# First MLP's weight halves kept in DRAM, and a float64 narrowing that takes its sign from a parametric ReLU

## The chip, the cores and the metric

The kernel runs on one core of one Trainium2 chip. A core has TensorE (PE, the matrix engine; PEld is its weight load), VectorE (DVE), ScalarE (ACT), GpSimd (POOL) and SyncE (SP), which issues all of this kernel's DMAs on one queue. Each engine works its instructions off in the order in which they were laid down, and semaphores tie the engines together. The metric is the time of one execution on the device in microseconds (us); the kernel before has a median of 1067.25 us over 3 runs (1065.96 to 1068.76).

## The reference, cut to what matters

```python
def _attn_ref(q_l, k_l, v_l, q_g, k_g, v_g):      # 4 batches, 8 heads, 512 local + 32 global tokens, head 64
    ...                                            # local window of 32 and global tokens, softmax
def _moe_ref(x, w_gate, w_val, w_out, rms_g):      # 2304 tokens, 512 wide, 1536 hidden
    rms = np.sqrt(np.mean(x * x, axis=-1, keepdims=True) + 1e-06)
    xn = x / rms * rms_g
    g = xn @ w_gate
    silu = g * (1.0 / (1.0 + np.exp(-g)))
    val = xn @ w_val
    return (silu * val @ w_out).astype(np.float32)
def _moe2_ref(x, w_in, w_out):                     # 512 wide, 2048 hidden
    h = x @ w_in
    g = np.maximum(0.01 * h, h)
    return (g @ w_out).astype(np.float32)
```

Attention, then a gated MLP, then a second MLP with a leaky ReLU. The weights of both MLPs come as float64 numbers; everything else is float32.

## The kernel before, in words

Each large matmul is done as three in the type float32r: every float32 operand is *split* into a high half (a rounding cast) and a low half (the operand minus the high half), and `mm3` (line 68) adds up high·high, low·high and high·low. `split` (line 85) makes a weight's high half on ACT (line 75) and its low half on POOL (line 83); the low halves of activations are made on DVE from the second block on, in the first block on POOL.

A float64 weight must first become a float32. `narrow` (line 93) gets the raw words of a 128x512 tile. ACT scales the upper word, read as a float32, by a power of two (line 104, tile `nc`, function Copy). DVE or POOL makes three low bits from the lower word (lines 109 and 106, tile `nr`). DVE shifts `nc` left by three and ORs the bits in (line 111), and a further DVE instruction ORs the sign bit in (line 112, tile `wf`, or `wfb` for the second MLP).

The first MLP takes the 2304 tokens in five blocks (512 and four times 416), and in each block 12 steps, one for each 128 hidden units. Step g uses three weights: k = 0 the gate (`pg` matmuls), k = 1 the value (`pv`), k = 2 the output (`yp` matmuls, which run in the next step). Beside blocks 0, 1 and 2 run the matmuls and softmax of the attention of batches 1, 2 and 3; block 3 has nothing beside it; block 4 has `ahead`: 12 weights of the second MLP are narrowed and split, and the first rows of the second MLP's input are read back and split.

In block 0 `convert` (line 495) narrows weight (g, k), starts the raw fetch of the next step into the one buffer `w64k` of that k, and stores the narrowed float32 tile `wf` to `w1_dram` (line 508). Blocks 1 to 4 fetch that tile (line 493, 256 KB) instead of narrowing again. In every block `prep` (line 510) then splits `wf` into the tiles `w0h`, `w0l` and so on, each with two buffers. `prep(g + 1, ...)` runs in step g, so a weight is split one step ahead and fetched two steps ahead.

The second MLP takes the tokens in five blocks with 16 steps each (`ph` matmuls, then `o`); between them ACT and DVE make `tl` and its halves `h2h` and `h2l`. All its 32 weights stay in the on-chip memory (SBUF). `weights2` (line 575) fetches, narrows and splits one: 12 in `ahead`, through three raw buffers, the other 20 in the second MLP's first block, through the two buffers of the tag `w64`.

The order on each engine is laid down by a scheduler that the program's order and its own estimate of time steer.

Of the kernel before, what the change touches and what calls it, by code (L numbers as in the profile page):

```python
# [8 lines left out]
F32 = mybir.dt.float32  # L9
F32R = mybir.dt.float32r  # L10
U32 = mybir.dt.uint32
AF = mybir.ActivationFunctionType
ALU = mybir.AluOpType
# [3 lines left out]
P = 128  # L17
# [6 lines left out]
def tile_window_global_attention_two_mlps(  # L24
# [10 lines left out]
    nc = tc.nc  # L35
    B, NP = kqv.shape[:2]
    _, _, KB, NT, _ = v_b.shape
# [6 lines left out]
    DM = NP * P  # L44
    KC = NP
    NF1 = w1.shape[0]
# [5 lines left out]
    scale = 1.0 / float(D) ** 0.5  # L52
# [4 lines left out]
    pools = [ph_ps.enter_context(tc.tile_pool(name="ps0", bufs=1, space=PSUM)), 8]  # L57
    dram = ctx.enter_context(tc.tile_pool(name="dram", bufs=1, space=bass.MemoryType.DRAM))
    y_dram = dram.tile([P, KC, NTOK], F32, name="y_dram")
    w1_dram = [[dram.tile([P, DM], F32, name=f"w1_dram{k}_{f}") for k in range(3)] for f in range(NF1)]  # L60
    ph1 = ctx.enter_context(ExitStack())
    mp = ph1.enter_context(tc.tile_pool(name="mp", bufs=1))
    ph_at = ExitStack()
# [9 lines left out]
    def high(eng, hi, src):  # L73
        if eng == "act":
            return nc.scalar.copy(hi, src)  # L75
        elif eng == "pool":
            nc.gpsimd.tensor_scalar(out=hi, in0=src, scalar1=1.0, scalar2=0.0, op0=ALU.mult, op1=ALU.add)
        else:
            nc.vector.tensor_copy(hi, src)
# [5 lines left out]
    def split(hi, lo, src, e_hi, e_lo):  # L85
        high(e_hi, hi, src)
        low(e_lo, lo, src, hi)
# [5 lines left out]
    def narrow(pool, dst, raw, name, e_r="dve"):  # L93

        c = pool.tile([P, DM], F32, tag="nar_c", bufs=2, name="nc_" + name)
        r = pool.tile([P, DM], U32, tag="nar_r", bufs=2, name="nr_" + name)
        cu = c.bitcast(U32)
        nc.scalar.activation(out=c, in_=raw[:, :, 1].bitcast(F32), func=AF.Copy, scale=2.0 ** -112)
        if e_r == "pool":
            nc.gpsimd.tensor_scalar(out=r, in0=raw[:, :, 0], scalar1=0.93 * 2.0 ** -29, scalar2=0.03,
                                    op0=ALU.mult, op1=ALU.add)
        else:
            nc.vector.tensor_scalar(out=r, in0=raw[:, :, 0], scalar1=2.0 ** -29, scalar2=7.0,  # L109
                                    op0=ALU.mult, op1=ALU.min)  # L110
        nc.vector.scalar_tensor_tensor(out=r, in0=cu, scalar=3, in1=r, op0=ALU.logical_shift_left, op1=ALU.bitwise_or)  # L111
        nc.vector.scalar_tensor_tensor(out=dst.bitcast(U32), in0=cu, scalar=0x80000000, in1=r,  # L112
                                       op0=ALU.bitwise_and, op1=ALU.bitwise_or)

    anchors = {}

# [360 lines left out]
    NI = len(BLOCKS1)  # L477
    wraw, wf, wsp = {}, {}, {}

    def step_of(g):  # L480
        return divmod(g, NF1)

    def fetch(g, k):

        i, f = step_of(g)
        if i >= NI:
            return
        if i == 0:
            wraw[g, k] = mp.tile([P, DM, 2], U32, tag=f"w64{k}", name=f"w64{k}_{f}")
            nc.sync.dma_start(out=wraw[g, k], in_=words(w1[f])[:, k])  # L490
        else:
            wf[g, k] = mp.tile([P, DM], F32, tag=f"wf{k}", bufs=2, name=f"wf{k}_{g}")
            nc.sync.dma_start(out=wf[g, k], in_=w1_dram[f][k])

    def convert(g, k):
        i, f = step_of(g)
        if i:
            return
        wf[g, k] = mp.tile([P, DM], F32, tag=f"wf{k}", bufs=2, name=f"wf{k}_{g}")
        with pinned({0: f"n{2 * NP - 1}", 1: "sqrt"}.get(f, "")):  # L500
            narrow(mp, wf[g, k], wraw[g, k], f"{k}_{f}", "pool" if k and f > 1 else "dve")
        if step_of(g + 1)[0] == 0:
            if g == 0:
                with tc.issue_after(loads[5, 1].ins):
                    fetch(g + 1, k)
            else:
                fetch(g + 1, k)
        nc.sync.dma_start(out=w1_dram[f][k], in_=wf[g, k])

    def prep(g, k):  # L510

        if step_of(g)[0] < NI:
            wsp[g, k] = [mp.tile([P, DM], F32R, tag=f"w{k}{y}", bufs=2, name=f"w{k}{y}_{g}") for y in "hl"]
            split(wsp[g, k][0], wsp[g, k][1], wf[g, k], "act", "pool")
        convert(g + 1, k)
        if step_of(g + 2)[0]:
            fetch(g + 2, k)

    cols = [sum(BLOCKS1[:i]) for i in range(NI)]
    yp = {}  # L520
# [75 lines left out]
    def mlp1(early):  # L596
# [8 lines left out]
        for g in range(NI * NF1):  # L605
            i, f = step_of(g)
# [4 lines left out]
            raw = g == 0  # L611
# [23 lines left out]
            for k in range(2):  # L635
                pp[k] = bank(f"p{'gv'[k]}_{g}")
                for c in range(KC):
                    mm3(pp[k][:, 0:n], [w[:, c * P:(c + 1) * P] for w in wsp[g, k]], [y[:, c, 0:n] for y in x],
                        c == 0, c == KC - 1)
                    if c == 1:  # L640
                        flush()
                        if k == 0:
                            prep(g, 2) if g else None
                        else:
                            prep(g + 1, 0)
                        between(2 * k)
                flush()
                if k == 0:
                    th = mp.tile([P, NX], F32, tag="th", bufs=2, name=f"th_{g}")
                    hs = [mp.tile([P, NX], F32R, tag=f"hs{y}", bufs=2, name=f"hs{y}_{g}") for y in "hl"]  # L650
                    t, hh, hl = (z[:, 0:n] for z in [th] + hs)
                    gate = pp[0][:, 0:n]
                    if raw:
                        gate = mp.tile([P, NX], F32, tag="gate", name="gate")[:, 0:n]
                        nc.vector.tensor_tensor(out=gate, in0=pp[0][:, 0:n], in1=norms[0][3]["rv"][:, 0:n], op=ALU.mult)
                    nc.scalar.activation(out=t, in_=gate, func=AF.Tanh, scale=0.5)  # L656
                    nc.vector.scalar_tensor_tensor(out=t, in0=t, scalar=1.0, in1=gate, op0=ALU.add, op1=ALU.mult)  # L657
                else:
                    nc.vector.scalar_tensor_tensor(out=t, in0=t, scalar=0.5, in1=pp[1][:, 0:n], op0=ALU.mult, op1=ALU.mult)
                    if raw:  # L660
                        nc.gpsimd.tensor_tensor(out=t, in0=t, in1=norms[0][3]["rv"][:, 0:n], op=ALU.mult)
                    high("act", hh, t)
                    later(lambda t=t, hh=hh, hl=hl: low("pool" if i < 1 else "dve", hl, t, hh))
                between(2 * k + 1)
            for m in range(2):
                if pend:
                    out_half(*pend, 2 * m)
                else:
                    flush()
                if m == 0:  # L670
                    prep(g + 1, 1)
                between(4 + m)
            pend = (g, [hh, hl])
        return pend
# [133 lines left out]
```

## Time and profile before

| | |
|---|---|
| median of 3 runs | 1067.25 us |
| the profiled execution | 1066.59 us |
| its span, first to last instruction | 1064.8 us |
| PE busy | 1002.9 us, 94% |
| DVE busy | 597.2 us, 56% |
| ACT busy | 481.4 us, 45% |
| POOL busy | 367.8 us, 35% |
| DMA moved | 116.33 MB, 109 GB/s over the span |
| granted PE clock, mean over the span | 0.977 of 2.4 GHz |

The profile shows one execution. For each engine it has the busy time, the time of each instruction, and for each idle time the instruction whose semaphore ended it ("hsl waits for hsh"). A line of a helper, such as 83, stands for many tiles, so a group is named by the tile it writes. Busy time of PE is that of matmuls which overlap: two that follow each other at 187 ns are shown with some 350 ns each, so PE's pace is read from counts in a stretch.

By the tiles, block 0 runs from about 57 to 219 us, blocks 1 to 3 to about 560 us, block 4 to 666 us, and the second MLP from there to the end.

### The profile page before, as it was taken

The numbers are of one execution on the slowest core, as the hardware profiler recorded it, in microseconds if no ns is written. First come the engines' busy times: TensorE is split into PE (matmuls) and PEld (weight loads), VectorE is DVE, ScalarE is ACT, GpSimd is POOL, SyncE is SP. The second block draws the span as 40 slices with busy tenths as digits, with TensorE's granted clock in tenths as the row PEclk, the third lists the DMA queues.
The fourth block names the chain that finished last, engine by engine and source line by source line (L and its number), as shares of the span: only waits on it lengthen the run. The fifth ranks groups of instructions, "written<-read, shape, count | busy, mean of one in ns | idle before, by whom it ended". The sixth has DMA issues, their size and how long they took to land.

```text
span 1064.8 us, 14868 instructions
## 1 busy us (share of the span) xinstructions
PE 1002.9 (94%) x5324; PEld 846.6 (80%) x5324; DVE 597.2 (56%) x1104; ACT 481.4 (45%) x1111; POOL 367.8 (35%) x283
## 2 busy tenths in 40 slices
PE   5968889999999999999997789988999999999998
PEld 4736667778888888899997689866888888888997
DVE  5899987366553866446349963599322232232232
ACT  4765556465554655455446543455222232232232
POOL 2468654543334443346557664244000000000000
PEclk8978999999999999999998999999999999999999
DMA  7556876633334442225345641453010010010000
GB/s 226 169 172 216 299 225 198 200 109 126 113 114 125 122 114 70 78 82 151 119 110 183 213 121 38 151 167 110 25 51 1 1 65 1 0 50 1 1 31 21
DMA packets 55452, 116.33 MB, mean 109 GB/s; under 512 B 8657, under 2 KB 11729, under 8 KB 55377
## 3 DMA queue, kind: packets, MB, share of 16 engines
q1 hardware_dynamic: 55376, 115.37, 34.6%
q8 instruction: 42, 0.69, 0.3%
q14 instruction: 34, 0.27, 0.1%
HBM read 97.00 MB, written 18.35 MB: 108 GB/s over the span
## 4 chain that ended last, share of the span: by engine, by line
PE 71%; DVE 7%; issue 4%; DMA 3%; ACT 1%; POOL 1%; DVEq 0%; SPq 0%; ACTq 0%
PE ph L71 15%; PE o L71 15%; PE yp L71 11%; PE pg L71 11%; PE pv L71 10%; PE po L257 2%; PE sc L213 2%; DMA w64b<-w 2%; PE pp L245 2%; DVE nr_b L109 1%; DVE wfb L112 1%; PE pz_g L320 1%; PE sa_g L279 1%; DVE nr_b L111 1%; DVE xl L83 1%
## 5 line engine op out<-in xcount | busy, mean ns | idle before, releaser
L733 DVE TENSOR_TENSOR tl<-ph,tl 128x512 f32<-128x512 f32 (+2 forms) x80 | 48.7, 609 | 153.8 <-ACT tl L732 153.5
L83 POOL TENSOR_TENSOR w0l<-wf,w0h 128x512 fp32r<-128x512 f32 x60 | 86.9, 1448 | 120.8 <-ACT w0h L75 116.8
L71 PE MATMUL ph<-ysph,w0l 128*128 128x512 f32 (+2 forms) x320 | 115.6, 361 | 0.0
L71 PE MATMUL ph<-yspl,w0h 128*128 128x512 f32 (+2 forms) x320 | 115.4, 360 | 0.0
L71 PE MATMUL ph<-ysph,w0h 128*128 128x512 f32 (+2 forms) x320 | 115.2, 360 | 0.0
L732 ACT ACTIVATE tl<-ph 128x512 f32<-128x512 f32 (+2 forms) x80 | 42.6, 533 | 160.1 <-PE ph L71 157.8
L83 POOL TENSOR_TENSOR w2l<-wf,w2h 128x512 fp32r<-128x512 f32 x60 | 88.2, 1470 | 70.7 <-ACT w2h L75 70.2
L71 PE MATMUL o<-w1h,h2l 128*128 128x512 f32 x272 | 107.6, 396 | 3.6 <-DVE h2l L83 3.5
L71 PE MATMUL o<-w1l,h2h 128*128 128x512 f32 x272 | 106.7, 392 | 0.0
L83 POOL TENSOR_TENSOR w1l<-wf,w1h 128x512 fp32r<-128x512 f32 x60 | 82.0, 1366 | 64.7 <-ACT w1h L75 58.6
L71 PE MATMUL pg<-xh,w0h 128*128 128x416 f32 (+1 forms) x236 | 90.2, 382 | 11.8 <-ACT w1h L75 7.2
L71 PE MATMUL yp<-hsh,w2h 128*128 128x416 f32 (+1 forms) x240 | 92.3, 389 | 4.8 <-ACT hsh L75 4.8
L71 PE MATMUL pg<-xh,w0l 128*128 128x416 f32 (+1 forms) x236 | 87.9, 372 | 2.3 <-POOL w0l L83 2.3
L71 PE MATMUL yp<-hsh,w2l 128*128 128x416 f32 (+1 forms) x240 | 89.5, 373 | 0.0
L71 PE MATMUL yp<-hsl,w2h 128*128 128x416 f32 (+1 forms) x240 | 81.7, 370 | 7.8 <-DVE hsl L83 7.8
L71 PE MATMUL o<-w1h,h2h 128*128 128x512 f32 x272 | 84.1, 398 | 5.0 <-ACT h2h L75 5.0
L71 PE MATMUL pg<-xl,w0h 128*128 128x416 f32 (+1 forms) x236 | 87.6, 371 | 0.3 <-DVE xl L83 0.2
L71 PE MATMUL pv<-xh,w1h 128*128 128x416 f32 (+1 forms) x236 | 86.5, 367 | 0.0
L71 PE MATMUL pv<-xl,w1h 128*128 128x416 f32 (+1 forms) x236 | 84.9, 360 | 0.0
L71 PE MATMUL pv<-xh,w1l 128*128 128x416 f32 (+1 forms) x236 | 84.5, 358 | 0.0
L83 DVE TENSOR_TENSOR h2l<-tl,h2h 128x512 fp32r<-128x512 f32 (+2 forms) x80 | 49.4, 618 | 50.0 <-ACT h2h L75 48.5
L657 DVE SCALAR_TENSOR_TENSOR th<-th,pg 128x416 f32<-128x416 f32 (+1 forms) x59 | 35.5, 601 | 73.1 <-ACT th L656 73.1
(149 smaller groups left out, 2219.3 us busy)
## 6 DMA issues: line engine op xcount, KB each, us to landing
wf<-w_dram SPq DMA_DIRECT2D x144, 256.0 KB, 2.7
w<-w SPq DMA_DIRECT2D x36, 512.0 KB, 4.6
w64b<-w SPq DMA_DIRECT2D x32, 512.0 KB, 4.3
kq<-kqv SPq DMA_DIRECT2D x32, 352.0 KB, 4.2
w_dram<-wf SPq DMA_DIRECT2D x36, 256.0 KB, 3.3
va<-kqv SPq DMA_DIRECT2D x16, 256.0 KB, 3.5
out<-ob SPq DMA_DIRECT2D x16, 256.0 KB, 2.1
y_dram<-ys SPq DMA_DIRECT2D x16, 208.0 KB, 2.5
```

The lines of the kernel that those rows point to most:

```text
L71: nc.tensor.matmul(dst, lhs[a], rhs[b], start=first and i == 0, stop=last and i == 2)
L83: e.tensor_tensor(out=lo, in0=src, in1=hi.bitcast(F32), op=ALU.subtract)
L109: nc.vector.tensor_scalar(out=r, in0=raw[:, :, 0], scalar1=2.0 ** -29, scalar2=7.0, op0=ALU.mult, op1=ALU.min)
L111: nc.vector.scalar_tensor_tensor(out=r, in0=cu, scalar=3, in1=r, op0=ALU.logical_shift_left, op1=ALU.bitwise_or)
L112: nc.vector.scalar_tensor_tensor(out=dst.bitcast(U32), in0=cu, scalar=0x80000000, in1=r, op0=ALU.bitwise_and, op1=ALU.bitwise_or)
L213: nc.tensor.matmul(sc[j][:, i * KW:(i + 1) * KW], kq[r, 2 * KW + i * P:2 * KW + (i + 1) * P], kq[r, i * KW:(i + 1) * KW], start=True, stop ...
L245: nc.tensor.transpose(pp[:, n * P:(n + 1) * P], s[:, c0:c0 + P], ident)
L257: nc.tensor.matmul(po[d, i * P:(i + 1) * P], v[0:rows, t, d], hold[j][0:rows, (n + i) * P:(n + i + 1) * P], start=n == 0, stop=n == 2)
L279: nc.tensor.matmul(sa[0:G2, 2 * h * P:2 * (h + 1) * P], q, k, start=True, stop=True)
L657: nc.vector.scalar_tensor_tensor(out=t, in0=t, scalar=1.0, in1=gate, op0=ALU.add, op1=ALU.mult)
L732: nc.scalar.activation(out=tl[:, 0:n], in_=pp[:, 0:n], func=AF.Copy, scale=0.01)
L733: nc.vector.tensor_tensor(out=tl[:, 0:n], in0=pp[:, 0:n], in1=tl[:, 0:n], op=ALU.max)
```

## The change

Three things. `narrow` loses the DVE instruction of line 112: ACT's function becomes a parametric ReLU with the slope −2^32 for negative inputs, so a negative number leaves it as a positive one with its exponent raised by 32, and the shift left by three moves that bit into the sign's place; line 111 then writes the result. In block 0 both halves of a weight lie in one tile of 128x2x512, and that tile (512 KB) is stored to DRAM, in `prep`, directly behind the split, no longer `wf` at the end of `convert`. In blocks 1 to 4 that tile is loaded ready (512 KB), at three places of step g for step g + 2, and nothing is split. The tile has three buffers for each k; the narrowed `wf` has one ring of five in place of two for each k.

```diff
-    w1_dram = [[dram.tile([P, DM], F32, name=f"w1_dram{k}_{f}") for k in range(3)] for f in range(NF1)]
+    w1_dram = [[dram.tile([P, 2, DM], F32, name=f"w1_dram{k}_{f}") for k in range(3)] for f in range(NF1)]
...
-        cu = c.bitcast(U32)
-        nc.scalar.activation(out=c, in_=raw[:, :, 1].bitcast(F32), func=AF.Copy, scale=2.0 ** -112)
+        nc.scalar.activation(out=c, in_=raw[:, :, 1].bitcast(F32), func=AF.Prelu, scale=2.0 ** -112,
+                             alpha=-2.0 ** 32)
...
-        nc.vector.scalar_tensor_tensor(out=r, in0=cu, scalar=3, in1=r, op0=ALU.logical_shift_left, op1=ALU.bitwise_or)
-        nc.vector.scalar_tensor_tensor(out=dst.bitcast(U32), in0=cu, scalar=0x80000000, in1=r,
-                                       op0=ALU.bitwise_and, op1=ALU.bitwise_or)
+        nc.vector.scalar_tensor_tensor(out=dst.bitcast(U32), in0=c.bitcast(U32), scalar=3, in1=r,
+                                       op0=ALU.logical_shift_left, op1=ALU.bitwise_or)
...
+    def weight_tile(g, k):
+
+        t = mp.tile([P, 2, DM], F32R, tag=f"w{k}", bufs=3, name=f"w{k}_{g}")
+        wsp[g, k] = [t[:, 0, :], t[:, 1, :]]
+        return t
+
     def fetch(g, k):
...
         else:
-            wf[g, k] = mp.tile([P, DM], F32, tag=f"wf{k}", bufs=2, name=f"wf{k}_{g}")
-            nc.sync.dma_start(out=wf[g, k], in_=w1_dram[f][k])
+            nc.sync.dma_start(out=weight_tile(g, k).bitcast(F32), in_=w1_dram[f][k])
+
+    def fetch_halves(g, k):
+        if step_of(g)[0]:
+            fetch(g, k)
 
     def convert(g, k):
         i, f = step_of(g)
         if i:
             return
-        wf[g, k] = mp.tile([P, DM], F32, tag=f"wf{k}", bufs=2, name=f"wf{k}_{g}")
+        wf[g, k] = mp.tile([P, DM], F32, tag="wf", bufs=5, name=f"wf{k}_{g}")
...
-        nc.sync.dma_start(out=w1_dram[f][k], in_=wf[g, k])
 
     def prep(g, k):
 
-        if step_of(g)[0] < NI:
-            wsp[g, k] = [mp.tile([P, DM], F32R, tag=f"w{k}{y}", bufs=2, name=f"w{k}{y}_{g}") for y in "hl"]
-            split(wsp[g, k][0], wsp[g, k][1], wf[g, k], "act", "pool")
-        convert(g + 1, k)
-        if step_of(g + 2)[0]:
-            fetch(g + 2, k)
+        i, f = step_of(g)
+        if i == 0:
+            t = weight_tile(g, k)
+            split(t[:, 0, :], t[:, 1, :], wf[g, k], "act", "pool")
+            nc.sync.dma_start(out=w1_dram[f][k], in_=t.bitcast(F32))
+            convert(g + 1, k)
...
                             prep(g + 1, 0)
+                        fetch_halves(g + 2, k)
                         between(2 * k)
...
                     prep(g + 1, 1)
+                else:
+                    fetch_halves(g + 2, 2)
                 between(4 + m)
```

## Rows read from the trace of the kernel before

**Rows 1.** The page: PE's busy us, share, instructions; then its tenths in 40 slices.

```profile
PE 1002.9 (94%) x5324; PEld 846.6 (80%) x5324; DVE 597.2 (56%) x1104; ACT 481.4 (45%) x1111; POOL 367.8 (35%) x283
...
PE   5968889999999999999997789988999999999998
```

**Rows 2.** Stretches: length, each engine's busy us (instructions), PE clock, DMA share, GB/s.

```profile
60.00:100.00 40.00, 29.57 (x125) 19.42 (x123) 39.74 (x65) 23.73 (x56) 28.09 (x20) 0.79 0.53 174
100.00:140.00 40.00, 36.70 (x195) 27.89 (x195) 39.22 (x70) 24.05 (x61) 28.58 (x19) 0.96 0.86 283
...
220.00:550.00 330.00, 329.57 (x1960) 292.45 (x1959) 186.60 (x402) 174.42 (x441) 144.21 (x108) 1.00 0.38 111
500.00:540.00 40.00, 40.00 (x214) 39.76 (x213) 14.79 (x19) 16.68 (x31) 23.55 (x19) 1.00 0.43 124
570.00:630.00 60.00, 42.71 (x200) 39.52 (x199) 52.92 (x56) 31.40 (x60) 45.15 (x32) 0.91 0.58 190
680.00:760.00 80.00, 71.45 (x292) 54.68 (x291) 64.44 (x85) 37.81 (x65) 30.60 (x20) 0.98 0.37 124
780.00:860.00 80.00, 80.00 (x347) 64.88 (x346) 20.80 (x32) 18.87 (x32) 0.00 (x0) 1.00 0.03 8
```

**Rows 3.** PE's waits, 550 to 760 us: us in total, times, longest.

```profile
PE yp L71 <- DVE hsl L83: 7.8, 5, 3.1
PE pg L71 <- ACT w1h L75: 7.2, 1, 7.2
```

**Rows 4.** Waits of the DMA queue (SP), the whole span.

```profile
SPq L493 <- POOL w0l L83: 121.1, 40, 8.4
...
SPq L578 <- DVE nr_b L109: 52.6, 23, 4.9
SPq L508 <- DVE wf L112: 43.5, 18, 6.9
```

**Rows 5.** Groups by shape: count, busy us, mean ns, idle before and its releasers.

```profile
L83 POOL TENSOR_TENSOR w0l<-wf,w0h 128x512 fp32r<-128x512 f32 x60 | 86.9, 1448 | 120.8 <-ACT w0h L75 116.8 <-DVE sq L433 3.2 <-POOL nr L106 0.6
...
L75 ACT CAST w0h<-wf 128x512 fp32r<-128x512 f32 x60 | 36.7, 611 | 0.0
...
L112 DVE SCALAR_TENSOR_TENSOR wf<-nc,nr 128x512 uint32<-128x512 uint32 x36 | 33.7, 950 | 6.8 <-POOL w2l L83 3.5 <-POOL w0l L83 2.9
...
L104 ACT ACTIVATE nc<-w 128x512 f32<-128x512 f32 x36 | 24.1, 672 | 28.4 <-issue 11.6 <-DVE wf L112 11.4 <-DMA w<-w 2.8
```

**Rows 6.** The tile hsl on DVE: ns min/median/max, first and last start.

```profile
L83 DVE TENSOR_TENSOR hsl<-th,hsh x48: 573/1274/1667, 237.9 to 665.6; 128x416 fp32r<-128x416 f32 x48
```

**Rows 7.** The page's DMA issues: count, size, median us from issue to landing.

```profile
w<-w SPq DMA_DIRECT2D x36, 512.0 KB, 4.6
w64b<-w SPq DMA_DIRECT2D x32, 512.0 KB, 4.3
```

**Rows 8.** DMA in 60 to 140 us: packets, the queue's share of 16 engines, issues.

```profile
DMA packets 6753, 18.28 MB, mean 229 GB/s; under 512 B 751, under 2 KB 751, under 8 KB 6746
...
q1 hardware_dynamic: 6746, 18.21, 69.3%
...
w_dram<-wf SPq DMA_DIRECT2D x20, 256.0 KB, 4.0
```

**Rows 9.** Groups of DVE in 570 to 630 us, columns as in rows 5.

```profile
L112 DVE SCALAR_TENSOR_TENSOR wfb<-nc_b,nr_b 128x512 uint32<-128x512 uint32 x10 | 13.2, 1315 | 2.4 <-POOL w0l L83 2.4
L109 DVE TENSOR_SCALAR nr_b<-w64b 128x512 uint32<-128x512 uint32 x8 | 11.4, 1421 | 0.0
```

**Rows 10.** DVE in order of time: start, us, instruction, idle before it.

```profile
680.53 0.43 DVE L109 TENSOR_SCALAR nr_b<-w64b 128x512 uint32<-128x512 uint32 x1 [3.97 <-DMA w64b<-w]
```

**Rows 11.** Groups of DVE in 680 to 742 us.

```profile
L112 DVE SCALAR_TENSOR_TENSOR wfb<-nc_b,nr_b 128x512 uint32<-128x512 uint32 x20 | 20.1, 1006 | 0.0
```

**Rows 12.** Groups of DVE in 60 to 140 us.

```profile
L112 DVE SCALAR_TENSOR_TENSOR wf<-nc,nr 128x512 uint32<-128x512 uint32 x21 | 19.7, 951 | 0.1
```

**Rows 13.** Groups by shape again: ACT's table loads ahead of Sqrt.

```profile
L461 ACT ACT_TABLE_LOAD x5 | 6.4, 1283 | 2.8 <-PE pm L458 2.7
```

## The prediction

> **What bounds the kernel now.** I read the page's busy shares first: TensorE (PE) is busy 94% of the span, so PE sets the time and only its idle time can be won. Its busy tenths fall below 9 in slices 1, 3 to 6, 22 to 24, 27 and 28 (and at the end) [rows 1]; those are the places to look at. The table of stretches gives the sizes [rows 2]. From 220 to 550 us (blocks 1 to 3 of the first MLP) PE idles 0.43 us of 330: nothing is to be had there. Three stretches fall short:
> - Block 0, where the first MLP's weights are narrowed beside attention: PE idles 10.4 us in 60 to 100 us and 3.3 us in 100 to 140, 13.7 together, while DVE is busy 79 of the 80 us.
> - Block 4, where the second MLP's first weights are narrowed: 570 to 630 us runs 200 matmuls. The undisturbed pace of the same shape is 214 in 40 us (500 to 540), 187 ns each, so the 200 are worth 37.4 us: 22.6 us are lost.
> - The second MLP's first block, with 20 more narrowings: 680 to 760 us runs 292 matmuls. The pace of 780 to 860 is 347 in 80 us, 231 ns each: 67.3 us of work, 12.7 us lost.
>
> Then what PE waits for between 550 and 760 us [rows 3]: the longest names are DVE's hsl and ACT's w1h. The first is DVE work served in its turn; the second is a split, fed by a fetch in the DMA queue, whose largest wait on POOL is 121.1 us for the low half w0l [rows 4]. So what stalls PE is two lists of work, DVE's and POOL's, that are served in order, and not the weights' bytes.
>
> **Part 1: a narrowing has one DVE instruction less (L112 goes), and ACT's Copy becomes Prelu.** Each of the first MLP's 36 takes 950 ns, 34 us of DVE together [rows 5]; the 32 of the second MLP are counted below by stretch. The trace has no Prelu. The nearest row is the Copy it replaces, 672 ns [rows 5]; the cast on the same 128x512 shape takes 611 [rows 5], so functions lie some 60 ns apart. I take no difference, with bounds of −60 and +60 ns: 2 us either way over 36, on an ACT that is busy 24 of 40 us [rows 2].
>
> **Part 2: blocks 1 to 4 load finished halves.** Removed: 48 × 3 = 144 splits. Of w0 the trace has 60 (12 of block 0, 48 later), 611 ns on ACT and 1448 ns on POOL [rows 5], and w1 and w2 have a group like it each: 88 us of ACT and 208 us of POOL go. In blocks 1 to 3 neither is on PE's path, so the gain there is 0. What the splits cost shows on DVE: hsl, with two operands in SBUF, takes 573 ns at least and 1274 in the median [rows 6], and DVE is busy only 14.8 of 40 us in block 3 [rows 2], so it isn't its own queue; I take it that a POOL split beside it holds it up, the other engine that reads the same memory then. PE covers that in block 3, not in block 4.
>
> Added: each load moves 512 KB, not 256: 144 × 262,144 B = 37.7 MB. Block 3 is the tightest: 3 × 524,288 B in a step of 36 matmuls × 187 ns = 6.73 us. In 500 to 540 us the DMA engines' share is 0.43 at 124 GB/s [rows 2], 288 GB/s when full, so a step's loads take 5.5 us of 6.73 and fit. With three buffers a load for step g+2 starts once step g−1 has released its tile: a lead of two steps, 13.5 us, against a landing of 4.6 us for 512 KB [rows 7]. Cost 0, covered by that lead; what it costs without is a rival below. The load waits for PE's reads now, no longer for POOL; in the SP queue behind it stand the stores of y and the raw loads, which have no reader in that step.
>
> **Part 3: block 0 stores the halves.** 36 stores grow by 262,144 B, 9.4 MB. They also move: from behind the next raw fetch to ahead of it, directly behind the split. SP then waits for POOL's low half, where it now waits for DVE's wf (43.5 us in 18 waits [rows 4]). Queued behind that wait are the raw fetch and the attention's loads. The raw fetch has to wait for the narrowing that reads its buffer, and on ACT that stands behind the same split, so I take 0 for the wait; the bytes are costed below.
>
> **The sum, stretch by stretch.**
> Block 4. DVE works 52.9 us in 570 to 630 [rows 2]. Ten of L112, at 1315 ns [rows 9], are 13.2 us of it. POOL runs 32 instructions there [rows 2]; about ten are splits of the second MLP (one for each of these narrowings) and stay, two thirds go. The 8 nr_b at 1421 ns [rows 9] took 430 ns undisturbed [rows 10], so 7.9 us of them is lengthening; two thirds, 5.3, go too. DVE falls to about 34 us, under the 37.4 us of matmuls, so PE becomes the bound. The turn in DVE's list still delays some steps: I leave 5.6 of 22.6. Gain 17, bounds 12 (L112 alone) and 22.6.
> The second MLP's first block. Twenty of L112 at 1006 ns [rows 11] leave DVE's 64.4 us [rows 2]. The next thing late is the ring of two w64 buffers: a landing of 4.3 us [rows 7] and a read of 0.7 (nc [rows 5]) make 5.0 us for two, 2.5 each, 50 us for 20 where 680 to 742 us are spent now. So DVE's 20 us can't all come back: 12 at most, and as DVE will wait for DMA with tl and h2l queued behind, I take 8. Bounds 4 and 12.7.
> [...]
> Block 0. 21 of L112 at 951 ns [rows 12], 20 us, leave a DVE that is full in 60 to 140 us: DVE alone would allow all 13.7 us. DMA moved 18.28 MB there at a share of 69.3% [rows 8], 330 GB/s when full. The 20 stores among it [rows 8] add 5.2 MB; 23.5 MB take 71 us, so at most 9 us of the 80 can go. In 100 to 140 us, with a share of 0.86 [rows 2], there is no room. I take 7, mostly in 60 to 100 us. Bounds −8 (a third of the 26 us that 33 × 262,144 B take at 330 GB/s) and 13.7.
> All else 0. Together 17 + 8 + 7 = 32 us. The profiled execution took 1066.59 us, 1.8 more than its span and 0.7 less than the median: 1067.25 − 32 = 1035 us.
>
> **The rivals.**
> *Block 0 becomes a DMA stage.* For it: 0.86 in 100 to 140 us. Against: 0.53 just before. Block 0 gains between 0 and −8, the ring only 4: 1067 − 17 − 4 + 4 = 1050, between 1043 and 1059.
> *Everything comes back.* DVE's turn no longer hurts anywhere: 22.6 + 12.7 + 13.7 = 49, 1018.
> *The store ahead of the raw load (slower).* In block 0 both run on one queue, and the store is issued first. Its 512 KB need what a 512 KB load needs, 4.6 us, so each raw load lands that much later; the raw buffers are single, so the next narrowing starts later too. It decides from the point where a landing of 9.2 us and the narrowing behind it (about 3 us: nr, L111, split) exceed the step, which would be some 12 us. Then 11 steps cost up to 4.6 us each: 1067 − 25 + 51 = 1093. Against: the engines were idle 30% of 60 to 140 us, and 9.2 + 3 only just reaches 12.
> *Halves late.* In block 4 raw loads at the SP queue's head wait up to 4.9 us for DVE's nr_b [rows 4]. Two in a row and 5.5 us of loading pass the lead of 13.5; seven times 4 us would eat block 4's gain and more: about 1065. Against: DVE, which holds them, is set free.
> *Prelu needs a table of its own, so the instruction saved on DVE is paid on ACT.* ACT reloads its table 5 times at L461, for Sqrt (as often again at L656), 1283 ns each [rows 13]. Two reloads for each narrowing are 2.57 us. In 680 to 760 us 20 × 2.57 = 51 on ACT's 37.8 make 89 of 80 us; in 60 to 140, 21 × 2.57 = 54 on 48 make 102 of 80: 1067 + 9 + 22 = 1098. For it: no row of Prelu. Against: Copy, Exp and Tanh alternate here without a reload. (The Trainium skill, "ScalarE: Activation LUTs", on table sets, names relu, copy, identity and abs as fillers of every set and not the parametric ReLU; no run here shows which holds.)
>
> **How the numbers follow.** Forecast (1022 to 1043) 0.62; DMA stage 0.15; everything back 0.09; store ahead of load 0.07; tables 0.04; halves late 0.03. The range of 1016 to 1059 leaves out the last three and a little of the others, 0.16. About 0.3% is what a measurement of this kernel can tell from no change. Slower: 0.07 + 0.04 = 0.11. Same: 0.03. Faster: 0.86.
>
> **What would show it.** L111 writes wf; POOL's splits of the first MLP end with block 0, and hsl takes 0.6 us from block 1 on; 570 to 630 us runs near 53 matmuls in 10 us with DVE below 80%; the DMA share is near 0.8 in block 3; in the second MLP's first block DVE's waits are for w64b. Wrong would be: PE waits for w0, w1 or w2 from DMA after block 0; more than 11 table loads; block 0's steps as long as now.

## The result, and the profile after

The changed kernel took 1037.72 us (median of 4 runs, 1035.93 to 1039.55) beside 1066.61 us for the kernel before (median of 4): a ratio of 0.9728, 95% interval 0.9703 to 0.9753. The profiled execution of after took 1037.57 us with a span of 1035.8, 29.0 us less than the span of before.

Both programs issue the same matmuls in the same order, so the start of the n-th matmul into pg (first MLP) or ph (second MLP) can be compared in the two traces. That puts the gain in its place. In before block 1 starts so at 227.4 us, block 4 at 562.4, the second MLP at 666.4 and its second block at 764.8. The table gives, for each stretch, how much shorter (minus) it is than in before, in us and good to 0.1; the columns of the experiments are used further down.

| stretch | after | e1 | e2 | e3 | e5 | e6b | e6 | e7 | e8 | g1 | g3 |
|---|---|---|---|---|---|---|---|---|---|---|---|
| up to the start of block 1 | −6.6 | −5.5 | −2.9 | −6.2 | −6.8 | −6.6 | −6.3 | −5.3 | −5.0 | −6.7 | −7.5 |
| blocks 1 to 3 | +1.6 | +0.7 | +1.5 | +5.4 | +2.3 | +2.1 | +1.1 | +0.3 | +1.0 | +7.2 | −2.4 |
| block 4 | −20.6 | −7.4 | −20.7 | −11.6 | −20.6 | −20.6 | −20.5 | −15.8 | −22.7 | −18.8 | −22.6 |
| second MLP's first block | −3.3 | −2.2 | 0.0 | −4.0 | −3.1 | −6.7 | −5.2 | −1.8 | −3.6 | −12.8 | −12.8 |
| sum | −28.9 | −14.4 | −22.1 | −16.4 | −28.2 | −31.8 | −30.9 | −22.6 | −30.3 | −31.1 | −45.3 |

After the second MLP's first block the distance stays the same to the end. Some seven tenths of the gain lie in block 4.

The page of after, PE's busy time and its tenths in 40 slices, answers to [rows 1]:

```profile
PE 994.5 (96%) x5324; PEld 843.7 (81%) x5324; DVE 506.7 (49%) x1036; ACT 404.6 (39%) x967; POOL 157.0 (15%) x139
...
PE   5967999999999999999999999979999999999998
```

The slices below 9 of block 4 are gone (22 to 24 in [rows 1]), and of the second MLP's two one is left. POOL has 144 instructions less, which is the 144 splits of blocks 1 to 4. The stretches of after answer to [rows 2] (length, busy us and instructions of each engine, PE clock, DMA share, GB/s):

```profile
60.00:100.00 40.00, 25.34 (x111) 17.43 (x110) 39.17 (x59) 25.44 (x58) 30.63 (x22) 0.76 0.70 245
100.00:140.00 40.00, 40.00 (x234) 30.97 (x234) 28.24 (x62) 25.34 (x65) 23.65 (x21) 0.99 0.97 359
220.00:550.00 330.00, 328.85 (x1956) 292.53 (x1955) 153.97 (x397) 117.27 (x333) 1.28 (x1) 1.00 0.59 195
500.00:540.00 40.00, 40.00 (x214) 39.76 (x213) 10.61 (x18) 6.35 (x12) 0.00 (x0) 1.00 0.74 237
570.00:630.00 60.00, 59.27 (x315) 58.38 (x314) 32.66 (x50) 21.18 (x40) 11.71 (x9) 1.00 0.86 321
680.00:760.00 80.00, 75.63 (x315) 59.76 (x315) 39.83 (x53) 31.18 (x54) 15.16 (x11) 0.98 0.25 84
```

570 to 630 us now runs 315 matmuls, not 200: with 321 at the undisturbed pace of 187 ns, 1.1 us are lost where 22.6 were. DVE's 32.66 us there are close to the 34 of the prediction, but they serve 315 matmuls and not 200, and hsl, whose shortening the 34 leaves out, is in them: that agreement is in part luck. The granted TensorE clock, 0.91 there before [rows 2], is 1.00; 0.09 of 60 us, some 5 us by this estimate, are the clock's part in what block 4 lost. It had fallen to 1.2 GHz in PE's wait of 7.2 us [rows 3] and stood there from 578 to 585 us. Block 0 shows the opposite of what was forecast for its parts: 60 to 100 us does less (PE 25.34 us, 29.57 before), 100 to 140 is full, and the DMA engines move 359 GB/s there.

The tile hsl on DVE in after, answering to [rows 6] (ns least/median/most), then groups of ACT by shape, answering to [rows 5] and [rows 13]:

```profile
L83 DVE TENSOR_TENSOR hsl<-th,hsh x48: 571/593/1675, 230.4 to 640.0; 128x416 fp32r<-128x416 f32 x48
```

```profile
L104 ACT ACTIVATE nc<-w 128x512 f32<-128x512 f32 x36 | 23.7, 666 | 9.1 <-DVE wf L112 4.7 <-DMA w<-w 2.1 <-issue 1.6
...
L461 ACT ACT_TABLE_LOAD x5 | 6.4, 1283 | 2.3 <-PE pm L458 2.2
L665 ACT ACT_TABLE_LOAD x5 | 6.4, 1283 | 6.6 <-PE pg L71 6.5
L226 ACT ACT_TABLE_LOAD x1 | 1.3, 1283 | 0.7 <-PEq L806 0.7
```

The median of hsl fell from 1274 to 593 ns. Prelu takes 666 ns where Copy took 672, and there are eleven table loads in all, as before: nothing reloads for Prelu. The page's DMA issues (count, KB each, median us to landing) answer to [rows 7], and the DMA view of 60 to 140 us to [rows 8]:

```profile
w<-w_dram SPq DMA_DIRECT2D x144, 512.0 KB, 4.0
w<-w SPq DMA_DIRECT2D x36, 512.0 KB, 6.4
w_dram<-w SPq DMA_DIRECT2D x36, 512.0 KB, 5.3
w64b<-w SPq DMA_DIRECT2D x32, 512.0 KB, 4.4
```

```profile
DMA packets 7012, 24.16 MB, mean 302 GB/s; under 512 B 790, under 2 KB 790, under 8 KB 7005
...
q1 hardware_dynamic: 7005, 24.08, 83.5%
```

The raw loads of block 0 land 1.8 us later than before (6.4 against 4.6). The waits of PE in 550 to 760 us, answering to [rows 3]; no load of halves stands among them:

```profile
PE o L71 <- DVE h2l L83: 3.2, 5, 1.1
PE o L71 <- ACT h2h L75: 2.6, 3, 1.6
PE pg L71 <- DVE th L666: 0.7, 1, 0.7
PE yp L71 <- DVE hsl L83: 0.7, 1, 0.7
```

### The profile page after: what moved, and what is told of

It is laid out like the page before. It is cut to its first block, busy times and chain, and to the rows that moved or that the text cites. A ratio compares the mean times of both kernels' runs of the same rounds, so it can differ in the third digit from the quotient of the medians.

```text
span 1035.8 us, 14249 instructions
## 1 busy us (share of the span) xinstructions
PE 994.5 (96%) x5324; PEld 843.7 (81%) x5324; DVE 506.7 (49%) x1036; ACT 404.6 (39%) x967; POOL 157.0 (15%) x139
## 4 chain that ended last, share of the span: by engine, by line
PE 51%; issue 35%; DVE 7%; DMA 5%; ACT 2%; POOL 0%; SPq 0%; DVEq 0%; ACTq 0%; POOLq 0%
PE o L71 16%; PE ph L71 16%; PE yp L71 5%; PE pv L71 5%; PE pg L71 4%; DMA w64b<-w 3%; PE po L257 1%; PE sc L213 1%; PE pp L245 1%; DVE wf L112 1%; DVE wfb L112 1%; DMA w<-w 1%; PE sa_g L279 1%; DVE nr_b L110 1%; DVE xn L469 1%
## 5 line engine op out<-in xcount | busy, mean ns | idle before, releaser
L71 PE MATMUL pg<-xh,w 128*128 128x416 f32 (+1 forms) x472 | 135.8, 367 | 7.2 <-ACT xh L75 6.5
L71 PE MATMUL yp<-hsh,w 128*128 128x416 f32 (+1 forms) x480 | 135.6, 373 | 1.6 <-ACT hsh L75 1.5
L71 PE MATMUL pv<-xh,w 128*128 128x416 f32 (+1 forms) x472 | 133.6, 363 | 0.0
L71 PEld LDWEIGHTS yp<-hsh,w 128*128 128x128 f32 x480 | 89.5, 191 | 12.3 <-issue 4.3
L71 PEld LDWEIGHTS pg<-xh,w 128*128 128x128 f32 x472 | 87.3, 189 | 14.6 <-ACT xh L75 7.3
L71 PEld LDWEIGHTS pv<-xh,w 128*128 128x128 f32 x472 | 86.8, 188 | 6.1 <-issue 1.9
L71 PE MATMUL pg<-xl,w 128*128 128x416 f32 (+1 forms) x236 | 86.1, 365 | 1.2 <-POOL xl L83 1.2
L71 PE MATMUL pv<-xl,w 128*128 128x416 f32 (+1 forms) x236 | 84.9, 360 | 0.0
L71 PE MATMUL yp<-hsl,w 128*128 128x416 f32 (+1 forms) x240 | 81.1, 365 | 0.7 <-DVE hsl L83 0.7
L226 ACT ACTIVATE s_ring<-s_ring,mx 128x224 f32<-128x224 f32 x128 | 60.5, 475 | 45.3 <-DVE mx L223 45.0
L83 DVE TENSOR_TENSOR h2l<-tl,h2h 128x512 fp32r<-128x512 f32 (+2 forms) x80 | 50.0, 625 | 50.8 <-ACT h2h L75 49.3
```

Of the source, the lines that this page charges most:

```text
L71: nc.tensor.matmul(dst, lhs[a], rhs[b], start=first and i == 0, stop=last and i == 2)
L83: e.tensor_tensor(out=lo, in0=src, in1=hi.bitcast(F32), op=ALU.subtract)
L226: nc.scalar.activation(out=sp, in_=sp, func=AF.Exp, bias=mx[:, c:c + 1], scale=-1.0, accum_out=sm[:, c:c + 1])
```

## The experiments

### The two halves of the change, each alone (e1, e2)

e1 puts the new narrowing into the kernel before; weights are stored and split as there.

```
-        nc.scalar.activation(out=c, in_=..., func=AF.Copy, scale=2.0 ** -112)
+        nc.scalar.activation(out=c, in_=..., func=AF.Prelu, scale=2.0 ** -112, alpha=-2.0 ** 32)
...
-        nc.vector.scalar_tensor_tensor(out=r, in0=cu, scalar=3, in1=r, ...)
-        nc.vector.scalar_tensor_tensor(out=dst.bitcast(U32), in0=cu, scalar=0x80000000, in1=r, ...)
+        nc.vector.scalar_tensor_tensor(out=dst.bitcast(U32), in0=c.bitcast(U32), scalar=3, in1=r, ...)
```

> The kernel before with the narrowing's change alone (one DVE instruction less, Prelu); blocks 1 to 4 still fetch wf and split. Theory (DVE's list is the stall, in all three stretches): block 0 gains 7 to 9 us, block 4 about 12, the second MLP's first block 3, so about 1043 us. Rival (block 4 is stalled by POOL's splits and the fetches that wait for them): block 4 gains under 5, about 1052 us.

e2 is the reverse: the changed kernel with the narrowing of before.

> The changed kernel with the narrowing of before (Copy and the two DVE instructions), so the halves alone are changed. Theory (DVE's list): block 4 gains 8 to 12 us since only the lengthening of DVE's instructions goes, block 0 loses 0 to 3 by the larger stores, the second MLP's first block 0; about 1057 us. Rival (POOL's splits): block 4 gains 17 to 20, about 1048 us.

Measured: e1 1051.96 us (ratio 0.9857, 0.984 to 0.9873), e2 1044.34 us (0.979, 0.9776 to 0.9805). 570 to 630 us in e1, then in e2:

```profile
570.00:630.00 60.00, 51.25 (x244) 49.26 (x245) 46.81 (x48) 34.28 (x65) 50.77 (x34) 0.91 0.63 199
```

```profile
570.00:630.00 60.00, 58.55 (x310) 57.51 (x309) 41.60 (x65) 23.48 (x45) 13.77 (x10) 1.00 0.91 331
```

The halves alone bring the whole of block 4 (−20.7 us of −20.6), though DVE keeps its second OR and is busy 41.6 us. The narrowing alone brings 7.4: POOL is then busy 50.8 of 60 us and DVE still 46.8. So in block 4 it was the splits, and not the number of DVE's instructions, that cost PE most of its time. In block 0, where the splits stay in all three, it is the other way about: 5.5 by narrowing, 2.9 by halves. Alone the two gain 14.9 and 22.5 us on the 1066.87 of their shared runs of before, 37.4 together, and 28.9 when made at once: in block 4 the second finds nothing left.

How POOL's splits reach DVE is to be seen in e1 in order of time, first DVE, then POOL (start us, length us, instruction):

```profile
590.29 0.68 DVE L111 SCALAR_TENSOR_TENSOR wfb<-nc_b,nr_b 128x512 uint32<-128x512 uint32 x1
590.98 1.60 DVE L83 TENSOR_TENSOR hsl<-th,hsh 128x416 fp32r<-128x416 f32 x1
592.51 1.52 DVE L109 TENSOR_SCALAR nr_b<-w64b 128x512 uint32<-128x512 uint32 x1
593.95 1.78 DVE L111 SCALAR_TENSOR_TENSOR wfb<-nc_b,nr_b 128x512 uint32<-128x512 uint32 x1
```

```profile
590.30 1.83 POOL L83 TENSOR_TENSOR w2l<-wf,w2h 128x512 fp32r<-128x512 f32 x1
592.10 1.64 POOL L83 TENSOR_TENSOR w1l<-wfb,w1h 128x512 fp32r<-128x512 f32 x1
593.70 1.48 POOL L83 TENSOR_TENSOR w2l<-wf,w2h 128x512 fp32r<-128x512 f32 x1
```

The two engines take turns. hsl starts at 590.98 while POOL works at w2l, and ends at 592.58, 0.45 us after w2l has ended; nr_b starts while POOL works at w1l (to 593.74) and ends 0.29 us after it. An instruction of 0.58 or 0.43 us takes 1.5 to 1.6 when a POOL subtraction was ahead of it. Over the whole run of before, the 11 hsl that start while POOL is idle take 573 to 593 ns, and the 37 that start while it works 731 to 1667. (The Trainium skill, "SBUF — State Buffer", section "Who interferes with whom", says that DVE and GpSimd share one pair of ports, held by one of them for a whole instruction, which a DVE instruction with two inputs in SBUF or a tensor_scalar can need. These rows agree: nr_b, a tensor_scalar, takes 1.52 us here and 0.43 alone [rows 10].)

### POOL's subtractions put back without a reader (e3) and taken off POOL (e7)

e3 adds to the changed kernel, after each load of halves, a subtraction on POOL that nobody reads.

```
+            if (g, k) in wsp:
+                h, l = wsp[g, k]
+                d = mp.tile([P, DM], F32, tag="wf", bufs=5, name=f"dummy{k}_{g}")
+                nc.gpsimd.tensor_tensor(out=d, in0=h.bitcast(F32), in1=l.bitcast(F32), op=ALU.subtract)
```

> The changed kernel, and in blocks 1 to 4 POOL subtracts one half of each loaded weight from the other into a tile that nobody reads: 144 instructions with two operands in SBUF, on no path. Theory (a POOL split beside a DVE instruction with two operands in SBUF holds it up): hsl's median goes from 593 back to about 1270 ns, and block 4 loses 5 to 10 us, about 1045 us. Rival (what counted was the wait for the splits' results): hsl may lengthen, the time stays within 3 us of the changed kernel's, 1038 us.

Measured: 1050.69 us (0.9862, 0.9832 to 0.9893), 13.0 us more than the changed kernel. Its 570 to 630 us:

```profile
570.00:630.00 60.00, 53.17 (x267) 51.51 (x266) 47.94 (x52) 23.74 (x45) 49.49 (x35) 0.94 0.88 319
```

DVE is busy 47.9 us with 52 instructions for 267 matmuls, where after had 32.7 us with 50 for 315. Block 4 loses 9 of its 20.6 us and blocks 1 to 3 lose 3.8 more, though no engine reads what these subtractions write. (The DMA queue waits for one of them four times in block 4, 3.0 us in all, before it loads into the buffer that was read; PE waits for no load there.) The median of hsl over the whole run stayed at 593 ns, against what was expected: the dummies start when a load lands, and in blocks 1 to 3 only 14 of 35 hsl start beside POOL's work, where 31 did in before. In 570 to 630 us its mean rose to 1117 ns (722 in after), and the OR's to 1199 (916).

From e1 to after block 4 gains 13.2 us, and POOL's subtractions alone take back 9.0. The other 4 aren't shown by themselves. PE's longest wait in block 4 of e1 is one that e3 doesn't have, for a split on ACT (w1h, 7.2 us, in before [rows 3]):

```profile
PE pg L71 <- ACT w2h L75: 5.1, 1, 5.1
```

So besides holding DVE up, the splits probably cost PE time directly, by being late.

e7 starts from e1 and moves block 4's 36 low halves from POOL to DVE.

```
-            split(wsp[g, k][0], wsp[g, k][1], wf[g, k], "act", "pool")
+            split(wsp[g, k][0], wsp[g, k][1], wf[g, k], "act", "dve" if step_of(g)[0] == NI - 1 else "pool")
```

> Narrowing alone (the one-OR narrowing on the kernel before), and in block 4 the low halves of the first MLP's weights are subtracted on VectorE, not on GpSimd: 36 subtractions more on VectorE, 36 fewer on GpSimd, the same loads. In narrowing alone 570 to 630 us showed GpSimd busy 50.8 us, VectorE 46.8 us with hsl at 1515 ns, the OR at 1190 ns and nr_b at 1166 ns, and TensorE 51.3 us. Theory A (a GpSimd subtraction and a VectorE instruction with two inputs in SBUF, or a tensor_scalar, hold each other up; it is this, not the amount of VectorE's work, that costs TensorE block 4): hsl goes back to some 580 to 700 ns, the OR to about 800, VectorE does more in the same time, and block 4 gains some 10 to 18 us on narrowing alone, so about 1035 to 1042 us. Theory B (the amount of VectorE's work): 36 times 0.68 us more on VectorE, block 4 is as long as with narrowing alone or longer, 1052 us or above.

Measured: 1041.65 us (0.9774, 0.976 to 0.9788), 10.3 us faster than e1 with more work on the engine that had looked like the bound. 570 to 630 us in e7, then two of DVE's groups there:

```profile
570.00:630.00 60.00, 56.95 (x289) 55.27 (x290) 50.64 (x78) 36.30 (x68) 17.27 (x10) 0.97 0.62 199
```

```profile
L83 DVE TENSOR_TENSOR w0l<-wf,w0h 128x512 fp32r<-128x512 f32 x10 | 7.9, 793 | 0.0
...
L83 DVE TENSOR_TENSOR hsl<-th,hsh 128x416 fp32r<-128x416 f32 x9 | 5.2, 580 | 0.0
```

DVE runs 78 instructions in 50.6 us where e1 ran 48 in 46.8, and hsl is back at 580 ns from 1515. That is theory A, at the low end of its range: in the trace block 4 gains 8.4 us on e1, under the 10 to 18 of the theory (the profiled execution, 1044.22 us, was the slowest of four). On before it is 15.8 us, not the 20.6 that come when the splits are gone altogether; DVE's own list, 50.6 of 60 us, is the likely reason and wasn't tried.

### Writes on POOL (e4)

Three memsets on POOL for each loaded weight, in the place of e3's subtraction.

```
...
+                for v in (1.0, 2.0, 3.0):
+                    nc.gpsimd.memset(d, v)
```

> The changed kernel, and in blocks 1 to 4 POOL sets such a tile three times for each loaded weight (some 1.5 us, no operand read): 432 instructions that only write. Theory (what holds DVE up is POOL's reading): hsl's median stays near 593 ns, time 1038 us. Rival (any POOL instruction beside it does): hsl's median 900 ns or more and about 1045 us.

Measured: 1205.72 us (1.1305, 1.1288 to 1.1322). As a test of its question it failed: the memsets wait for nothing, so 376 of the 432 ran back to back at the start of block 1, where e3's subtractions are spread, and hsl ran beside none of them. What it showed instead stands in the last section.

### Is block 0 held by its transfers? (e5)

```
-            nc.sync.dma_start(out=weight_tile(g, k).bitcast(F32), in_=w1_dram[f][k])
+            nc.sync.dma_start(out=weight_tile(g, k).bitcast(F32), in_=w1_dram[0][k])
...
-            nc.sync.dma_start(out=w1_dram[f][k], in_=t.bitcast(F32))
+            if f == 0:
+                nc.sync.dma_start(out=w1_dram[f][k], in_=t.bitcast(F32))
```

> The changed kernel with 33 of its 36 stores of halves left out: only the first of the 12 weight pairs is stored, and the later blocks load that pair's halves for every step, so their products are not the reference's. All instructions on TensorE, VectorE, ScalarE and GpSimd stay. It asks what holds block 0 (60 to 220 us), whose DMA share with the stores is 0.97 in 100 to 140 us. The prediction's theory (VectorE's and GpSimd's list sets the order, and the stores lie behind the raw loads): block 0 gains 1 to 3 us, about 1036 us. Rival (block 0's DMA stage, the prediction's first rival): the raw loads land sooner, block 0 gains as far as narrowing alone did not, 6 us or more, about 1030 us or below.

Measured: 1036.95 us (0.9717, 0.9702 to 0.9732), no different from the changed kernel. The DMA engines are relieved, and PE is not:

```profile
60.00:100.00 40.00, 25.90 (x111) 18.01 (x111) 38.67 (x59) 24.74 (x54) 29.84 (x22) 0.76 0.56 188
100.00:140.00 40.00, 40.00 (x237) 30.98 (x234) 31.27 (x68) 28.91 (x76) 27.55 (x24) 0.97 0.75 234
```

Block 1 starts 0.2 us earlier than in after, which is neither the 1 to 3 us of the theory nor the 6 of the rival, though the raw loads land in 4.4 us and not in 6.4. Neither the bytes of the stores nor their place ahead of the raw loads cost block 0 anything that this shows, though the share in 100 to 140 us was 0.97 with them.

### What holds the second MLP's first block? (e6b, e6, e8)

e6 gives the raw weights w64 three buffers. There was no room in SBUF for a third, so nc is written into wf, and e6b is that step alone.

```
-        c = pool.tile([P, DM], F32, tag="nar_c", bufs=2, name="nc_" + name)
+        c = dst if in_place else pool.tile([P, DM], F32, tag="nar_c", bufs=2, name="nc_" + name)
...
-        r = tmp.tile([P, DM, 2], U32, tag=tag, bufs=2 if tag == "w64" else 1, name=f"w64b{k}_{f}")
+        r = tmp.tile([P, DM, 2], U32, tag=tag, bufs=3 if tag == "w64" else 1, name=f"w64b{k}_{f}")
```

> The changed kernel with the second MLP's narrowing writing its nc into the buffer wf (the one OR then works in place), which frees no step of the chain and makes room in SBUF. It is the control of the next run. Both theories: the changed kernel's time, 1038 us within 2 us.

> The same with three buffers in place of two for the second MLP's raw weights. Theory (in its first block the two-buffer ring of raw weights is next late: a transfer can only start once VectorE has narrowed the weight two places earlier): the ring of three recovers most of the 6.3 us that TensorE still loses there, so about 1032 to 1034 us. Rival (VectorE's list itself, or the DMA engines' rate, sets it): 1038 us, with TensorE's loss in that block unchanged.

e8 takes DVE's work away instead.

```
-        narrow(tmp, wf, r, f"b{k}_{f}")
+        nc.scalar.activation(out=wf, in_=r[:, :, 1].bitcast(F32), func=AF.Prelu, scale=2.0 ** -112, alpha=-2.0 ** 32)
```

> The changed kernel with VectorE's share of the second MLP's 32 narrowings left out: ScalarE's Prelu writes wf directly, nr_b and the OR are not done, so the second MLP's weights are wrong by the factor 2^112 and in their last bits. Loads, ring of two, ScalarE's and GpSimd's instructions stay. A ring of three buffers had recovered nothing of the 6.3 us that TensorE loses in the second MLP's first block. Theory (VectorE's list, lengthened by GpSimd's subtractions, holds that block): 5 us or more of the 6.3 come back there and up to 2 in block 4, about 1030 to 1032 us. Rival (landing and the ring of w64 buffers hold it, as the prediction said): 48 to 50 us for the last 20 loads as before, 1036 to 1038 us.

Measured: e6b 1034.41 us (0.97, 0.9687 to 0.9713), e6 1035.69 us (0.971, 0.9697 to 0.9724), e8 1035.44 us (0.9705, 0.9691 to 0.9719). The queue's issue of the last 20 raw loads (start, us from the start of the first to the end of the last issue) in before, after, e6 and e8:

```profile
676.66 55.15 SPq L578 DMA_DIRECT2D w64b<-w  x20
```

```profile
651.08 47.93 SPq L586 DMA_DIRECT2D w64b<-w  x20
```

```profile
650.96 48.65 SPq L586 DMA_DIRECT2D w64b<-w  x20
```

```profile
649.95 46.26 SPq L586 DMA_DIRECT2D w64b<-w  x20
```

and these stretches in e6 and in e8:

```profile
651.00:699.00 48.00, 43.96 (x185) 33.93 (x184) 38.79 (x48) 26.40 (x46) 21.69 (x16) 1.00 0.62 207
```

```profile
651.00:697.00 46.00, 40.60 (x168) 30.84 (x167) 10.96 (x12) 28.71 (x48) 22.38 (x18) 0.99 0.67 217
```

With DVE's part left out, DVE is idle three quarters of the time, and the loads still take 46 us. The first two find their buffers free; the other 18 start 2.5 us apart, which is a landing of 4.3 us (the median of these 20) and a Prelu of 0.67, shared by two buffers. That is the ring of the prediction.

With three buffers the loads take as long as with two, and DVE is busy 38.8 of 48 us. What held them then e6 doesn't settle. Its nc lies in wf, which has two buffers, so the Prelu that frees a raw buffer has to wait for wf; and the queue waits longer for this Prelu than for DVE:

```profile
SPq L586 <- ACT wfb L104: 30.1, 17, 2.5
SPq L586 <- DVE nr_b L110: 8.1, 7, 2.7
```

So both theories were half wrong. DVE's list and the ring are late by almost the same time (47.93 us with both, 46.26 with the ring alone), and to take away the list shows the ring. The other way about isn't shown: no run took away the ring, or both, with nothing put in its place.

Nor is the length of the loads the whole of what PE loses here. In the control e6b they take 49.58 us, longer than in after, and the block is 3.4 us shorter, which wasn't expected. PE waits in this block for no weight but for h2h and h2l, the halves that ACT and DVE make between the narrowings: 5.8 us in after, 3.5 in e6b, 5.1 in e6, 5.4 in e8. A part is the clock. 680 to 760 us of e6b:

```profile
680.00:760.00 80.00, 76.72 (x325) 60.53 (x326) 41.12 (x56) 31.83 (x55) 14.79 (x12) 1.00 0.25 84
```

The granted clock is 1.00 there, and in e6, but 0.98 in after, which on 80 us is 1.6 us (an estimate): half of e6b's 3.4 us and most of e6's 1.9. Why e6b's order leaves PE fewer waits is open. And 6.3 us, which the expectations of these runs take as lost here, was too little: by the runs that follow there were 9.5 to win.

### A version that goes on from there (g1, g2, g3)

On the idea that narrowing costs nothing where PE is full, g1 treats the second MLP's 32 weights like the first MLP's: narrowed and split during blocks 1 to 3, halves stored, then loaded.

```
...
+                        if k and 1 <= i < 4:
+                            w2_make(g - NF1 - 1)
+                            for j in (0, 1) if g == NF1 else (g - NF1 + 1,):
+                                w2_fetch(j)
```

> The changed kernel, with the second MLP's weights treated the same way: during blocks 1 to 3 each of its 32 raw weights is loaded, narrowed and split between the first MLP's steps, its halves are stored to DRAM, and the second MLP loads halves alone. Theory (what still costs time is narrowing beside TensorE in block 4 and the second MLP's first block): that block loses nothing (minus 6.3 us), block 4 drops its remaining narrowing (minus 2 us), blocks 1 to 3 take the work in VectorE's and ScalarE's idle time at no cost: about 1029 us. Rival (narrowing and GpSimd's splits cost TensorE time wherever they stand, as they did in block 4 before): blocks 1 to 3 lengthen by 8 us or more, 1038 us or above.

Measured: 1029.57 us (0.9669, 0.9647 to 0.969; its profiled execution, from which the table's column is, took 1035.06). The second MLP's first block is 9.5 us shorter than in after, and blocks 1 to 3 are 5.6 us longer. Two stretches of g1 show where it pays:

```profile
220.00:260.00 40.00, 37.39 (x182) 29.20 (x181) 29.28 (x79) 22.53 (x64) 12.63 (x8) 0.91 0.98 348
...
590.00:600.00 10.00, 7.99 (x34) 7.43 (x33) 2.40 (x4) 1.05 (x2) 0.00 (x0) 0.83 1.03 408
```

The first steps of block 1 run 182 matmuls (238 in after); in 590 to 600 us PE waited 2.0 us for a load of halves while the DMA engines were full, and the clock granted in those 10 us was 0.83 in the mean, where the stretches around it had 1.00 (2.4 GHz). g2 starts the narrowing three steps later, subtracts on DVE, and issues six loads in block 4, not twelve; g3 is g2 with ten loads there:

```
-                        if k and 1 <= i < 4:
-                            w2_make(g - NF1 - 1)
+                        if k and i < 4 and g >= NF1 + 3:
+                            w2_make(g - NF1 - 4)
...
-            split(hl[0], hl[1], x, "act", "pool")
+            split(hl[0], hl[1], x, "act", "dve")
...
-        for f in range(6):
+        for f in range(5):
```

> The kernel that also stores the second MLP's halves, with three things moved: its narrowing starts three steps later in block 1 (the first steps there lost 7 us), its low halves are subtracted on VectorE, not on GpSimd, and 6 in place of 12 of its halves' loads are issued in block 4 (where the DMA share was 1.03 for 40 us and TensorE's clock fell to 0.83 for 10). Theory (those 7 us and the 2 us of block 4 came from GpSimd's subtractions, from work laid on the crowded first steps of a block, and from the burst of loads): blocks 1 to 3 go back to within 1 us of the changed kernel, the second MLP's first block keeps its gain of 9.5 us, together about 1027 us (the profiled run before was 1035, the median 1029.6), down to 1022. Rival (32 narrowings cost blocks 1 to 3 wherever they stand): 1029 us or above.

> The last combined version with 10 in place of 6 of the second MLP's loads issued in block 4. There the second MLP's first block still lost some 3 us in 640 to 660 us, where the other 26 loads start together and TensorE waited 2.0 us for one. Theory: with four more there in time that wait goes, about 1022 us. Rival (the burst of loads in block 4 costs as much again): 1025 us or above.

Measured: g2 1024.70 us (0.9609, 0.9596 to 0.9622), g3 1021.41 us (0.9574, 0.9561 to 0.9588), the fastest of all, 16.3 us below the changed kernel. In g2 the second MLP's first block is only 5.6 us shorter than in after, with a wait of PE of 2.0 us for a load of halves; in g3 it is 9.5 us shorter again. DVE's groups of the moved narrowing in g3, 250 to 520 us:

```profile
L84 DVE TENSOR_TENSOR wfcl<-wfc,wfch 128x512 fp32r<-128x512 f32 x21 | 14.3, 681 | 0.9 <-ACT wfch L76 0.8
L113 DVE SCALAR_TENSOR_TENSOR wfc<-nc_c,nr_c 128x512 uint32<-128x512 uint32 x20 | 13.7, 685 | 0.2
L111 DVE TENSOR_SCALAR nr_c<-w64c 128x512 uint32<-128x512 uint32 x18 | 7.6, 420 | 0.2
```

With POOL still, the OR takes 685 ns and nr 420, where they took 1315 and 1421 beside its splits [rows 9]. All 32 narrowings in blocks 1 to 3 cost no time there that shows: that stretch is even 4.0 us shorter than in after, and why isn't known. g2 changes three things at once, and no run parts them.

## Why the prediction came out right, point by point

The forecast of 1035 us was 2.7 us low, inside its own range; its terms are less good than its sum.

**Block 4: 17 us forecast, 20.6 measured; the reason was half wrong.** The term "L112 alone, 12 us" as the lower bound fell: narrowing alone gave 7.4 (e1). It counted ten instructions of 1315 ns as 13.2 us to be won, but such an instruction takes 0.68 us undisturbed, so about half of that length was POOL's turn. With L112 gone POOL ran more splits in the same time, 50.8 us of 60, and hsl kept a median of 1282 ns over the run. The other term, that a POOL split holds up a DVE instruction beside it, was taken as an assumption and is now shown (e3, e7). It was mis-sized: the prediction gives it 5.3 us of nr_b, where putting the subtractions back takes 9.0 us (e3) and removing the splits brings the whole gain with L112 still there (e2). The clock has no term of its own; its 5 us lie inside the 22.6 us that the prediction had as lost.

**The second MLP's first block: 8 us forecast, bounds 4 and 12.7; 3.3 measured.** The gain lies under the lower bound. The mechanism put as next late, the ring of two, is there, and at its price (e8: 2.5 us a load, 46.26 us for 20, forecast 50). What was mis-sized is the time it was held against: 62 us, from the stretch 680 to 742. The 20 loads themselves took 55.15 us before, which left 5 to win by that reckoning. The 12.7 us that were lost there are right: g1 and g3 win 12.8.

**Block 0: 7 us forecast, 6.6 measured; its place and the DMA rate were wrong.** The gain was to come in 60 to 100 us, with no room in 100 to 140. It came in 100 to 140 and after: the third step's first matmul is still 2.7 us late, the seventh's 8.0 us early. The step that failed is "330 GB/s when full", from a share and a mean over 80 us: with the stores the same stretch moves 24.16 MB at 83.5%, 362 GB/s by the same sum, and e5 shows that the DMA engines were no bound. The trace of before had it already: cut into 2 us, 60 to 140 us shows up to 412 GB/s. That DVE's list is what holds block 0 is borne out as far as e1 goes (5.5 us of the 6.6); the third step starts later in e1 too (5.8 us). In the step before it PE waits for ACT's xh, a half of the first MLP's input, which ends at 77 us in after: 4.5 us, 5.2 in e1, 1.1 in before. DVE makes its source xn later there, behind a narrowing; that this order is the reason wasn't tried.

**Blocks 1 to 3: 0 forecast, 1.6 us lost.** e2 has the same loss (1.5), e1 half of it, and in block 2 alone after is 1.9 us longer, e2 2.9 and e1 0.0; by that it goes with the halves. How is open. The loads themselves are on time: no wait of PE names them after block 0.

**Prelu, the halves' landing, the queue's order: 0 forecast, 0 found.** 666 against 672 ns; 4.0 us of landing against the lead of 13.5; the raw loads land 1.8 us later behind the stores, not the 4.6 of the slower rival, and e5 prices that at nothing. No rival decided anything: the eleven table loads stayed, and the DMA engines were full in 100 to 140 us (share 0.97) at no cost to PE that e5 shows.

The sum: 20.6 + 3.3 + 6.6 − 1.6 = 28.9 us against 32. That it came so near is partly luck: block 4's 3.6 us too few and the second MLP's 4.7 too many nearly cancel.

## What to carry to other kernels

An engine that looks full may be waiting inside its instructions: compare each group's mean with the shortest time of the same instruction, and look which engine is at work beside the long ones, before counting its instructions as time to be won. Work taken off that other engine, even off every path, can be worth more than work taken off the full one. And where two things are late by the same time, removing one shows little; what helped here was to move the work to a stretch with room.

## What the runs showed of the hardware

A DVE instruction of 4 elements a partition took 169 us, to the end of POOL's memsets; after them it takes 0.17. From e4, DVE, then POOL, then the wait of PE that came of it:

```profile
227.74 169.07 DVE L232 TENSOR_SCALAR sm<-sm 128x4 f32<-128x4 f32 x1
396.84 0.18 DVE L233 RECIPROCAL sm<-sm 128x4 f32<-128x4 f32 x1
```

```profile
221.23 175.55 POOL L507 MEMSET dummy<- 128x512 f32 x376
```

```profile
PE pp L245 <- DVE s_ring L235: 166.7, 1, 166.7
```

The memsets end at 396.78 us and the tensor_scalar at 396.81. It has one input, and a memset reads nothing. Beside subtractions the two engines alternated; here the instruction got no turn among memsets in an unbroken row. Not every DVE instruction is held: just before it ten others ran beside the memsets at their usual length (L223 0.39 us, th 0.58). That POOL's row held it is read off the two end times, and wasn't tried by itself.

The DMA engines moved 408 GB/s over 10 us at a share of 1.03 (g1, 590 to 600 us), well above the 330 that the prediction had taken for full.
